# wq's load cut into 16 and 112 partitions in a one-token decode kernel

## The chip, the cores and the metric

The kernel runs on one core of a Trainium2 chip. Five engines of the core take part: TensorE (PE), VectorE (DVE), ScalarE (ACT), GpSimd (POOL) and SyncE (SP). Sixteen DMA engines move data between the device memory and the core's memory of 128 partitions (SBUF). The metric is the device time of one execution in microseconds, the median of the runs; a profiled execution gives the trace.

## What is computed

Two sequences, one new token each (B = 2, Sq = 1, D = 512). A grouped attention over a cached context of 32,768 positions, and a small MLP whose result gates it:

```python
xn = layernorm(x)
q  = (xn @ wq)                  # 32 heads of 128, 8 of them in keys and values: 4 heads share one
p  = softmax(q . k_cache * 128**-0.5)
s  = (p . v_cache) @ wo
h  = mlp_in_and_shift(layernorm(xn), w1) @ w2    # the shifts leave only zeros where S = 1
x1 = xn + h
g  = silu(x1 + gelu(layernorm(x1) @ w3) @ w4)
out = x + s * g
```

All inputs are bf16. With one token, each shifted group of the MLP's first part is padded with zeros alone, so that w1 and w2 do not reach the result and the kernel does not load them. What has to be moved is the cache, 2 x 8 pairs of K and V of 8 MiB each (268 MB), and the weights: wq 4 MiB, w3 and w4 1.75 MiB each, wo 4 MiB.

## The kernel before

Two large buffers hold what is loaded. `kbuf` has three places of 32 KB a partition (`CW` elements each), `vbuf` two. A K tile takes two of kbuf's three places, and the tiles of even and odd units overlap in the middle one. At the start kbuf's third place holds wq and vbuf's first 28 KB hold w3; both are used up before K of unit 1 and the first half of V of unit 0 arrive in their place.

There are 16 units n (sequence n % 2, key head n // 2). For each, `scores` lets DVE transpose K in eight pieces (L488), and PE multiplies each by the unit's q (L500); `softmax` follows on DVE, PE and ACT (L513 to L530); `values` multiplies the probabilities by V on PE (L541), and `unit_sum` and `unit_out` collect the result. At the end come the gelu, w4, wo and the gate.

Ahead of the units, `q_job` makes q for all heads: PE multiplies xrep (the normalised x, spread over the array) by wq in 32 matmuls (L448), ACT copies the eight results out (L458), DVE transposes them (L463) and packs them into qp (L465), and POOL places a unit's part into qz (L474). `mlp_in` (L572) follows on PE and reads w3. xrep comes from x through the two layernorms, a pair of small loads (z4) and a transpose (L426, L429).

All instructions are recorded in one list an engine by the class `Plan`, which works out the waits: each operation names the regions that it reads and writes, and where two overlap, the later one waits for the semaphore of the earlier. A load adds 16 to its semaphore when it has landed. SP issues all the large loads in program order on one queue: wq, w3, the two halves of K of unit 0, the second half of V of unit 0 (L326 for each, which is the helper's line), then the first half of V after `mlp_in` has read w3, and from there K and V of the next unit as soon as their places have been read. ACT issues the four small loads of x and z4 on a queue of its own.

The first loads are written so:

```python
wq_v = A_wq.rearrange("(p k) f -> p k f", k=DK)
wq_s = kbuf[:, 2 * CW:3 * CW].rearrange("p (k f) -> p k f", k=DK)
load("wq", wq_s, wq_v, [kreg(2 * CW, CW)])
load("w3", w3_s, w3_v, [("vbuf", 0, W3)])
load_k(0)
load_v0_half(1)
```

Each partition's part of wq is 32 KB in one piece, on both sides.

Of the kernel before, what the change touches and what calls it, by code (L numbers as in the profile page):

```python
# [195 lines left out]
def kernel(  # L196
# [37 lines left out]
    CW = UT * Dh  # L234
# [4 lines left out]
    wq_v = A_wq.rearrange("(p k) f -> p k f", k=DK)  # L239
# [6 lines left out]
    def sb(name, shape, dt, align=32):  # L246
        return nc.alloc_sbuf_tensor(name, shape, dt, align_bytes=align).ap()
# [12 lines left out]
    xrep = sb("xrep", [128, DK, 4, 32], BF16)  # L260
# [52 lines left out]
    def al(name, lo=0, hi=1 << 30):  # L313
        return (name, lo, hi)

    def on(eng):
        def record(fn, rd=(), wr=(), label=None, times=None):
            P.op(eng, fn, [al(r) if isinstance(r, str) else r for r in rd],
                 [al(w) if isinstance(w, str) else w for w in wr], label=label, times=times)
        return record  # L320

    dve, act, pool, pe = on("DVE"), on("ACT"), on("POOL"), on("PE")

    def load(sem, out_ap, in_ap, wr, rd=(), eng="SP"):
        e = {"SP": nc.sync, "ACT": nc.scalar}[eng]
        P.op(eng, lambda: e.dma_start(out=out_ap, in_=in_ap), [al(r) if isinstance(r, str) else r for r in rd],  # L326
             [al(w) if isinstance(w, str) else w for w in wr], dma=sem)
# [10 lines left out]
    def kreg(lo, w):  # L338
        return ("kbuf", lo, lo + w)
# [18 lines left out]
    wq_s = kbuf[:, 2 * CW:3 * CW].rearrange("p (k f) -> p k f", k=DK)  # L358
    w3_s = vbuf[:, 0:W3].rearrange("p (k f) -> p k f", k=DK)
    w4_s = kbuf[:, 0:FK * D].rearrange("p (f d) -> p f d", f=FK)  # L360

    load("wq", wq_s, wq_v, [kreg(2 * CW, CW)])
    load("w3", w3_s, w3_v, [("vbuf", 0, W3)])
    load_k(0)

# [67 lines left out]
    def q_job():  # L433
        kb = kbuf[:, :]

        q_row, q_turn = (vbuf[:, W3 + HD * i:W3 + HD * (i + 1)] for i in range(2))

        def vreg(i, lo, w):
            return ("vbuf", W3 + HD * i + lo, W3 + HD * i + lo + w)

        spots = [("sc", 0, 512), ("sc", 512, 1024), "acc", "mA", "hP", "mD", "wP", "s_ps"]

        def fn(done):

            pes = [mybir.EngineType.PE]
            with nc.Fori(0, 2, 1, engines=pes) as e, nc.Fori(0, 4, 1, engines=pes) as h:
                for k in range(DK):
                    r = T.matmul(  # L448
                        banks[:, bass.ds(e * 2048 + h * 512, 512)],
                        lhsT=xrep[:, k, :, :].rearrange("p i w -> p (i w)"),  # L450
                        rhs=kb[:, bass.ds(h * 1024 + (e + (2 * CW + k * HD)), 1023)][:, 0:1023:2],
                        start=(k == 0), stop=(k == DK - 1))
                done(r)

        for c, spot in enumerate(spots):
            pe(None if c else fn, [kreg(2 * CW, CW), "xrep"], [spot], times=None if c else 8)
        for c, spot in enumerate(spots):
            act(lambda c=c: A.copy(  # L458
                out=q_row.rearrange("p (h x two w) -> p h two x w", h=4, two=2, w=32)[:, c % 4, c // 4, :, :],
                in_=banks[:, 512 * c:512 * (c + 1)].rearrange("p (x w) -> p x w", w=32)),  # L460
                [spot], [vreg(0, 1024 * (c % 4) + 512 * (c // 4), 512)])
        for c in range(0, 4096, 1024):
            dve(lambda c=c: V.transpose(out=q_turn[:, c:c + 1024], in_=q_row[:, c:c + 1024]),  # L463
                [vreg(0, c, 1024)], [vreg(1, c, 1024)])
        dve(lambda: V.tensor_copy(  # L465
            out=qp[:, :, :, :, :].rearrange("p k b g h -> p k b (g h)"),
            in_=q_turn.rearrange("p (h k b c) -> p k b h c", k=4, b=B, c=16)[:, :, :, :, 0]), [vreg(1, 0, HD)], ["qp"])

        for t, name in ((acc, "acc"), (mD, "mD"), (wP, "wP")):
            dve(lambda t=t: V.memset(t, 0.0), [], [name])  # L470
# [109 lines left out]
    def gelu():  # L580
# [9 lines left out]
        dve(lambda: V.transpose(out=h_bf[:, :], in_=h_row[:, :]), ["h_row"], ["h_bf"])  # L590

    q_job()
    place_q(0)
    mlp_in()
# [138 lines left out]
```

## Time and profile before

| | |
|---|---|
| median of 3 runs | 657.31 us (656.68 to 657.52) |
| profiled execution | 656.69 us, of which the span of the instructions 654.9 us |
| PE, DVE, ACT busy | 61%, 59%, 5% of the span |
| DMA | 280.55 MB, mean 428 GB/s over the span |
| mean granted clock of TensorE | 0.834 |

The profile is one execution, taken by the hardware profiler. Its page gives the busy time of each engine, the span in 40 slices, the DMA queues (q1 is SP's, q10 ACT's), the chain of work that ended last, the costliest groups of instructions by line, and the DMA issues with the time from issue to landing. The timeline lists instructions in order: start, duration, engine (SPq is SP's queue, where a duration is that of the issue), line, what is written and read, and in brackets how long the engine stood idle before and what ended that. Busy time by stretch gives for each stretch its length, the busy time and count of each engine, the granted clock, the share of the 16 DMA engines and their rate in GB/s.

### The profile page before, as it was taken

The page shows a single profiled execution, that of the slowest core. Times are in us where ns is not written, and L with a number is a line of the kernel's source. Part 1 is how long each engine was busy: PE and PEld are TensorE (multiplying, and loading weights), DVE is VectorE, ACT ScalarE, POOL GpSimd, SP SyncE. Part 2 cuts the span into 40 slices and gives each one's busy share as a digit, 9 for nine tenths or more (in the row PEclk, how much of TensorE's full clock was granted, in tenths as well). Part 3 has the DMA queues.
Part 4 walks back from the last instruction along what each step waited for, and adds up shares of the span by engine and source line. Part 5 has one row for each costly group of instructions (what it writes and reads, how often), then busy time and mean ns, then how long its engine had stood idle before and what let it go on. Part 6 is the DMA issues. An engine that isn't in the chain of part 4 may idle for free.

```text
span 654.9 us, 5862 instructions
## 1 busy us (share of the span) xinstructions
PE 397.9 (61%) x2297; PEld 152.0 (23%) x2297; DVE 384.6 (59%) x302; ACT 33.5 (5%) x67; POOL 7.6 (1%) x28
## 2 busy tenths in 40 slices
PE   0876183665648466573855658486464847646855
PEld 0222031221213222121321213122121312212322
DVE  4592381945739185572928548293763819367862
ACT  1201000000000000000000000000000000000011
POOL 1000000000000000000000000000000000000000
PEclk9997598886979878697887869787797977779988
DMA  8999999999999999999999999999999999999996
GB/s 360 448 424 466 400 448 444 448 416 420 448 444 436 404 444 444 448 416 420 448 444 444 396 445 444 448 424 412 448 444 444 404 436 444 448 428 406 450 411 278
DMA packets 6383, 280.55 MB, mean 428 GB/s; under 512 B 738, under 2 KB 748, under 8 KB 1260
## 3 DMA queue, kind: packets, MB, share of 16 engines
q1 hardware_dynamic: 6348, 280.50, 99.1%
q8 instruction: 2, 0.03, 0.0%
q10 hardware_dynamic: 32, 0.01, 0.0%
q14 instruction: 1, 0.01, 0.0%
HBM read 280.50 MB, written 0.00 MB: 428 GB/s over the span
## 4 chain that ended last, share of the span: by engine, by line
DMA 73%; DVE 14%; PE 7%; issue 5%; SPq 0%; DVEq 0%
DMA kbuf<-in_A_k_cache_dram 69%; DVE ktb L488 13%; PE banks L500 7%; DMA kbuf<-in_A_wo_dram 5%; DVE acs L551 1%; SPq L326 0%; DVE acr L555 0%; DVEq L90 0%; PE banks L654 0%; DVE sg L688 0%; DVE out_bf L689 0%; SPq L728 0%; SPq L693 0%
## 5 line engine op out<-in xcount | busy, mean ns | idle before, releaser
L488 DVE STREAM_TRANSPOSE ktb<-kbuf 128x2048 uint32<-128x2048 uint32 x128 | 286.8, 2286 | 172.9 <-DMA kbuf<-in_A_k_cache_dram 170.7
L500 PE MATMUL banks<-ktb,qz 128*128 128x512 bf16 x1024 | 268.2, 410 | 164.8 <-DVE ktb L488 164.1
L500 PEld LDWEIGHTS banks<-ktb,qz 128*128 128x128 bf16 x1024 | 95.6, 102 | 338.6 <-issue 189.6
L541 PE MATMUL banks<-vbuf,pT 128*16 128x512 bf16 x1024 | 90.6, 532 | 15.9 <-DVE rS L530 13.1
L541 PEld LDWEIGHTS banks<-vbuf,pT 128*16 128x16 bf16 x1024 | 31.8, 117 | 68.0 <-issue 56.8
L513 DVE TENSOR_REDUCE m<-banks 128x1 f32<-128x1024 f32 x16 | 19.6, 1225 | 32.0 <-PE banks L500 32.0
L529 DVE STREAM_TRANSPOSE pT<-pr 128x1024 bf16<-128x1024 bf16 x16 | 19.9, 1245 | 20.4 <-ACT pr L523 20.4
L565 ACT CAST oQ<-banks 128x4 bf16<-128x4 f32 x16 | 2.6, 162 | 519.8 <-PE banks L562 519.8
L526 PE MATMUL banks<-S,headf 128*128 128x1 f32 x32 | 7.8, 314 | 23.8 <-ACT pr L523 23.8
L448 PE MATMUL banks<-kbuf,xrep 128*128 x32 | 10.4, 480 | 16.8 <-DVE xrep L429 16.3
L523 ACT ACTIVATE pr<-banks,nb 128x1024 bf16<-128x1024 f32 x16 | 17.8, 1114 | 39.0 <-DVE nb L522 39.0
L555 DVE TENSOR_REDUCE acr<-acs 128x128 f32<-128x512 f32 x17 | 17.6, 1036 | 0.6
L514 PE MATMUL banks<-identf,m 128*1 128x128 f32 x16 | 4.3, 270 | 19.2 <-DVE m L513 19.2
L551 DVE SCALAR_TENSOR_TENSOR acs<-banks,rS,mask 128x512 f32<-128x512 f32 x17 | 12.1, 711 | 5.3 <-PE banks L541 5.3
L519 PE MATMUL banks<-ones_f,gx 1*128 1x1 f32 x32 | 6.4, 266 | 9.9 <-DVE gx L517 9.9
L526 PEld LDWEIGHTS banks<-S,headf 128*128 128x128 f32 x32 | 6.5, 252 | 25.2 <-ACT pr L523 25.2
L474 POOL TENSOR_TENSOR qz<-qp,qm 128x64 bf16<-128x64 bf16 x17 | 5.0, 293 | 621.3 <-PE banks L500 595.3
L463 DVE STREAM_TRANSPOSE vbuf<-vbuf 128x1024 bf16<-128x1024 bf16 x4 | 4.9, 1234 | 8.6 <-ACT vbuf L458 8.5
L448 PEld LDWEIGHTS banks<-kbuf,xrep 128*128 128x128 bf16 x32 | 3.6, 113 | 23.1 <-issue 21.4
L519 PEld LDWEIGHTS banks<-ones_f,gx 1*128 1x128 f32 x32 | 5.0, 196 | 13.0 <-DVE gx L517 13.0
L515 DVE TENSOR_REDUCE gm<-banks 1x4 f32<-1x128 f32 x16 | 4.5, 278 | 5.8 <-PE banks L514 5.8
L522 DVE TENSOR_SCALAR nb<-banks 128x1 f32<-128x1 f32 x16 | 2.5, 158 | 7.8 <-PE banks L519 7.8
(74 smaller groups left out, 61.0 us busy)
## 6 DMA issues: line engine op xcount, KB each, us to landing
kbuf<-in_A_k_cache_dram SPq DMA_DIRECT2D x4, 4096.0 KB, 27.0
vbuf<-in_A_v_cache_dram SPq DMA_DIRECT2D x2, 4096.0 KB, 35.6
kbuf<-in_A_wq_dram SPq DMA_DIRECT2D x1, 4096.0 KB, 13.4
kbuf<-in_A_wo_dram SPq DMA_DIRECT2D x1, 2048.0 KB, 33.6
vbuf<-in_B_w_dram SPq DMA_DIRECT2D x1, 1792.0 KB, 17.2
kbuf<-in_B_w_dram SPq DMA_DIRECT2D x1, 1792.0 KB, 29.9
kbuf<-in_A_wo_dram SPq DMA_DIRECT2D x1, 1024.0 KB, 32.1
kbuf<-in_A_wo_dram SPq DMA_DIRECT2D x4, 256.0 KB, 30.9
```

The source lines that it names most:

```text
L448: r = T.matmul(banks[:, bass.ds(e * 2048 + h * 512, 512)], lhsT=xrep[:, k, :, :].rearrange("p i w -> p (i w)"), rhs=kb[:, bass.ds(h * 1024 ...
L474: pool(lambda: G.tensor_tensor(out=qz[:, :, 32 - rep:].rearrange("p k (i w) -> p k i w", w=32)[:, :, :, 0:rep], in0=qp[:, :, b, g, :].unsq ...
L488: dve(lambda i=i, c0=c0: V.transpose(out=ktb[i][:, :], in_=kbuf[:, c0:c0 + KG * GT * Dh].bitcast(U32)), [kreg(c0, KG * GT * Dh)], [f"ktb{i ...
L500: r = T.matmul(sc[:, bass.ds(half, HW)].rearrange("p (t k) -> p t k", k=32), lhsT=qz[:, k, off:off + 128], rhs=kv[:, k // 2, k % 2, :, :], ...
L513: dve(lambda: V.tensor_reduce(out=m1[:, :], in_=sc[:, :], axis=AX.X, op=ALU.max), ["sc"], ["m1"], "max")
L519: pe(lambda: T.matmul(bc, lhsT=gx[:, :, :].rearrange("o x h -> o (x h)"), rhs=ones_f[0:1, 0:1], start=True, stop=True), ["gx", "ones_f"], ...
L523: act(lambda: A.activation(out=pr[:, :], in_=sc[:, :], func=ACT.Exp, bias=nb[:, 0:1], scale=inv_sqrt_dh, accum_out=S1[:, :]), ["sc", "nb"] ...
L526: pe(lambda: T.matmul(sS, lhsT=headf[:, :, :].rearrange("p x h -> p (x h)"), rhs=S1[:, :], start=True, stop=True), ["headf", "S1"], [rO], "S")
L529: dve(lambda: V.transpose(out=pT[:, :, :].rearrange("p t r -> p (t r)"), in_=pr[:, :]), ["pr"], ["pT"], "pT")
L541: r = T.matmul(acc[32 * j:32 * j + 16, :].rearrange("p (i d) -> p i d", d=Dh), lhsT=pT[:, half * GT + u, r0:r0 + 16], rhs=vv[:, x, u, :, : ...
L551: dve(lambda: V.scalar_tensor_tensor(out=acs[:, :, :], in0=acc[:, :].rearrange("p (i d) -> p i d", d=Dh), scalar=rS[:, 0:1], in1=mask[:, : ...
L555: dve(lambda: V.tensor_reduce(out=acr[:, :], in_=acs[:, :, :].rearrange("p i d -> p d i"), axis=AX.X, op=ALU.add), ["acs"], ["acr"], "acr")
```

## The change

The one load of wq becomes two on the same semaphore: the first 16 partitions, then the other 112. The first writes the region of kbuf as before; the second is recorded as writing a name of its own, "wq_rest", so that it does not wait for the first. The q matmuls name both, and so wait until the semaphore stands at 32 where it was 16. SP issues one instruction more; the lists of the other engines have the same instructions as before, and what SP issues after it keeps its order.

```diff
-    load("wq", wq_s, wq_v, [kreg(2 * CW, CW)])
+
+    for p0, p1, spot in ((0, 16, kreg(2 * CW, CW)), (16, 128, "wq_rest")):
+        load("wq", wq_s[p0:p1], wq_v[p0:p1], [spot])
     load("w3", w3_s, w3_v, [("vbuf", 0, W3)])
     load_k(0)
...
         for c, spot in enumerate(spots):
-            pe(None if c else fn, [kreg(2 * CW, CW), "xrep"], [spot], times=None if c else 8)
+            pe(None if c else fn, [kreg(2 * CW, CW), "wq_rest", "xrep"], [spot], times=None if c else 8)
```

## The prediction

> **What bounds the kernel now.** I read the page first (span, the DMA strip, the chain that ended last), then the chain in order of time, then busy time by stretch, and last the timeline of the first 45 us.
>
> ```profile
> span 654.9 us, 5862 instructions
> DMA  8999999999999999999999999999999999999996
> DMA packets 6383, 280.55 MB, mean 428 GB/s; under 512 B 738, under 2 KB 748, under 8 KB 1260
> q1 hardware_dynamic: 6348, 280.50, 99.1%
> DMA 73%; DVE 14%; PE 7%; issue 5%; SPq 0%; DVEq 0%
> ```
>
> The 16 DMA engines are busy in every slice but the first and the last, nearly all of it with the one queue of SP (q1), and the chain is 73% transfers. The rest of the chain, the DVE and PE pieces, could still be time in which the DMA engines stand still. The next view says that it is not.
>
> ```profile
> core 0: us, PE busy (x) PEld busy (x) DVE busy (x) ACT busy (x) POOL busy (x), PEclk, DMA share, GB/s
> 1.75:2.75 1.00, 0.00 (x0) 0.00 (x0) 0.20 (x1) 0.20 (x1) 1.00 (x5) 1.00 1.96 526
> 2.75:3.75 1.00, 0.00 (x0) 0.00 (x0) 1.00 (x1) 1.00 (x1) 0.82 (x1) 1.00 0.00 0
> 3.75:4.75 1.00, 0.00 (x0) 0.00 (x0) 0.93 (x3) 0.09 (x1) 0.00 (x0) 1.00 1.22 524
> 12.00:40.00 28.00, 18.07 (x67) 5.62 (x68) 16.67 (x17) 4.69 (x8) 0.30 (x1) 1.00 1.01 436
> 100.00:600.00 500.00, 310.05 (x1751) 119.22 (x1752) 294.30 (x207) 17.62 (x38) 3.52 (x12) 0.82 1.00 433
> ```
>
> The last column is the rate of the transfers. From 12 us on it is 436, and over the 500 us of the middle 433 GB/s: one rate, without pauses. 280.5 MB at 433 GB/s take 648 us of the 654.9; the other 7 us are the start and the end. So the transfers' stream bounds the kernel, and a microsecond lost or won in it is lost or won in the span, if the stream has always work in its queue. It has:
>
> ```profile
> 2.37 35.56 DMA kbuf<-in_A_k_cache_dram
> 41.69 34.90 DMA kbuf<-in_A_k_cache_dram
> 512.87 27.37 DMA kbuf<-in_A_k_cache_dram
> 619.89 31.13 DMA kbuf<-in_A_wo_dram
> 651.07 0.32 PE banks L654 x8
> ```
>
> A K load has 8.39 MB, 19.4 us at 433 GB/s. The one issued at 512.87 lands 27.37 us later, so 8.0 us of other work stood ahead of it; at 41.69 it was 34.90 - 19.4 = 15.5 us. The chain names the DVE between two K loads because DVE's reads release the next issue, but each issue comes 8 us or more before the engines need it. At the end PE needs 0.3 us after the last part of wo has landed: nothing there gives time back.
>
> **The change, part by part.** It cuts the first transfer of the program (wq, 128 partitions of 32 KB each) in two: partitions 0 to 15, then 16 to 127. Bytes, later loads and the instructions of the compute engines stay. One issue is added on SP, and the wait of PE ahead of the q matmuls counts both loads.
>
> ```profile
> 0.96 0.39 SPq L326 DMA_DIRECT2D kbuf<-in_A_wq_dram  x1
> 1.42 0.41 SPq L326 DMA_DIRECT2D vbuf<-in_B_w_dram  x1
> 2.90 28.17 SPq L326 DMA_DIRECT2D vbuf<-in_A_v_cache_dram  x2
> 14.35 0.38 DVE L425 CAST zb<-z 128x256 bf16<-128x256 f32 x1 [4.64 <-DMA z<-ktb]
> 15.25 0.29 DVE L429 COPY xrep<-zT 128x512 bf16<-128x512 bf16 x1
> 16.26 8.22 PE L448 MATMUL banks<-kbuf,xrep 128*128 x24 [16.26 <-DVE xrep L429]
> 31.06 4.47 DVE L488 STREAM_TRANSPOSE ktb<-kbuf 128x2048 uint32<-128x2048 uint32 x2
> 41.69 0.33 SPq L326 DMA_DIRECT2D kbuf<-in_A_k_cache_dram  x1
> kbuf<-in_A_wq_dram SPq DMA_DIRECT2D x1, 4096.0 KB, 13.4
> ```
>
> *One more issue on SP.* Two issues stand 1.42 - 0.96 = 0.46 us apart. The rest of wq, w3, both halves of K and the first half of V are issued 0.46 us later. The cover is the first row of each engine: 524 KB, 16 rows of 32 KB, at 433 GB/s are 1.21 us a row, and the first rows took about 2 (begun from 1.75 on, the second ones from 3.75 on, in the rows above). 0.46 is less than either, so I cost it at 0; without the cover it would be +0.46. The ACT queue's loads (x, x4, z4) are not behind it.
>
> *The start.* By quarters of a microsecond the first rows begin so:
>
> ```profile
> 1.75:2.00 0.25, 0.00 (x0) 0.00 (x0) 0.00 (x0) 0.00 (x0) 0.25 (x2) 1.00 1.08 270
> 2.00:2.25 0.25, 0.00 (x0) 0.00 (x0) 0.00 (x0) 0.00 (x0) 0.25 (x3) 1.00 5.02 1311
> 2.25:2.50 0.25, 0.00 (x0) 0.00 (x0) 0.00 (x0) 0.00 (x0) 0.25 (x1) 1.00 0.95 262
> 2.50:2.75 0.25, 0.00 (x0) 0.00 (x0) 0.20 (x1) 0.20 (x1) 0.25 (x2) 1.00 0.78 262
> ```
>
> A quarter at 262 GB/s is 65.5 KB, two rows; so 2, 10, 2 and 2 engines begin in the four quarters (the strip puts a packet's bytes where it begins). The four late ones are up to 0.75 us behind the first. A first load with one row for each engine may let them all begin together. That is worth 0 to 0.75 us, and only if a late one is also the one that ends last; I take -0.3.
>
> *The first 16 rows.* No row of this trace shows sixteen engines writing into sixteen neighbouring partitions, so I bound it. A single row is no limit: an engine puts 32 KB into one partition in 1.21 us. The 16 engines together write no faster than 16 rows in 1.21 us, and whether neighbours share a way into the memory can't be seen, since each load spreads over all 128 partitions. If no neighbours share, the 16 rows cost 1.21 us as now: +0. If the eight partitions that fall to an engine now (128 / 16) were neighbours with one way for all, 16 neighbours would have two ways and the rows would queue eight deep: 8 x 1.21 - 1.21 = +8.5 us for every engine. Between the ends lie two to a way (+1.2) and four to a way (4 x 1.21 - 1.21 = +3.6). The rows don't single one out, and the middle of the two ends, 4.2, is nearest to four to a way: I take +3.6 and keep both ends.
>
> [...]
>
> *The other 112 rows.* Seven rows for each engine, 7 x 1.21 = 8.5 us, as the last seven of eight now: +0 at best. At worst, in runs of seven, every row meets another engine's row on one way: 7 x 1.21 = +8.5. In the present load nobody waits (1.21 us a row, in the rate of 433 GB/s). Seven is no multiple of two, four or eight, so runs of seven would not line up with ways of that many neighbours, and some rows meet; the slowest engine counts, since a load has landed when its last engine is done. Nearest to the known end of no meeting I take one and a half rows, +1.8.
>
> *Does the lost time come back?* The sum so far makes the last engine 5.1 us late at the end of wq, and the rates above show no spare speed to catch up with. What waits for wq is PE at L448. wq lands at 0.96 + 13.4 = 14.4 and PE starts at 16.26, released by xrep (15.25 + 0.29); so 1.9 us are hidden, and with wq 5.1 us later PE starts about 3.2 us later. Behind it on PE wait the w3 matmuls, after them SP's issue of V's second half (the 28.17 us at 2.90 end at 31.07), and through q the transposes at 31.06 and the K issue at 41.69. All shift by some 3 us against 15.5 us of queued transfers: hidden. If that cover were gone, 3.2 us would be added instead of hidden. The z4 load, which lands at 14.35, has its rows among wq's and may be some late too; it shares the same cover.
>
> *Sum:* 0 - 0.3 + 3.6 + 1.8 = +5.1 us. The profiled execution took 656.69 us beside its span of 654.9; 656.69 + 5.1 = 661.8. It lies 0.6 under the median of the runs, 657.31, so the runs should give about 657.31 + 5.1 = 662.4 us, 0.8% slower. What a measurement of this kernel can tell from no change is about 0.2%, 1.3 us.
>
> **The rivals.**
>
> *The rows do not hinder each other and only the start counts.* Then 656.6 to 657.3 us: the -0.3 taken, at most -0.75. It decides when neighbours have ways of their own. For it: one row at a time runs at full rate into one partition. Against it: nothing in this trace, where no load is so narrow. Within 0.2%. To be faster by over 0.2% also the slow first rows have to shrink: 2.0 - 1.21 = 0.8 and the 0.75 of the spread, together -1.5 us, 655.8. The 2 us are the same for early and late engines, which speaks for a latency that a smaller load pays as well.
>
> *The small load isn't one row for each engine.* If an engine is tied to its partitions, 16 neighbours fall to few of the engines, and the others begin at once with the rest; each engine has its eight rows in all, as before, and the time is 657.3. For it: now every engine gets eight rows and none waits. [...]
>
> *The rest is dealt in turn, row by row.* Then each of its seven steps again puts 16 neighbours side by side, and each costs what the first 16 rows cost: 8 x 3.6 = +29 us, 686. Nothing in the trace shows how rows are dealt. With eight to a way in the first load alone, +8.5 + 1.8 - 0.3, it would be 667.3.
>
> **How the numbers follow.** Slower by 2 to 9 us through the narrow load: 0.57, its own range 659.5 to 666.5 (first load at two to eight rows deep, the rest at 0 to three rows). Much slower (rest in turn, or eight to a way): 0.09. No hindrance: 0.19 within 0.2% and 0.05 faster. Few engines: 0.10, same. That is faster 0.05, same 0.29, slower 0.66. The likeliest gives 662.4. With signs on both sides, a range for 8 in 10 must reach from the unhindered cases, 656.6, over the likeliest one's upper end to 667.0; outside are the 0.09, the 0.05 and a few hundredths of the edges.
>
> **What would show it.** Right: between about 2 and 7 us the rate falls to 100 to 200 GB/s, where it is now 526, 0 and 524 in single microseconds; wq lands near 19 us (its last part 18 after its issue); L448 starts near 19.5 released by the wq load and not by xrep; the middle stays at 433 GB/s; each K landing, and the last of wo, about 5 us later. Wrong: second rows starting from 3.75 to 4.75 as now. If the first rows show 5 us and wq lands 4 late but the span grows less, the stream had slack that I did not see; if it grows by far more than wq is late, some engines ran dry, or the wait at L448 reached the K issue.

## The result and the profile after

The changed kernel took 665.39 us, the median of 4 runs (664.53 to 665.86), against 657.37 for the kernel before in the same sitting: 8.0 us more, a ratio of 1.0126 with a 95% interval of 1.0114 to 1.0138. The forecast was 662.4 with a range of 656.6 to 667.0. Two of the four runs of `probe_far`, below, took 736.6 us at a lower granted clock (0.79 to 0.80, where its other two had 0.82); they are left out and not explained.

The profiled execution took 665.81 us, its span is 664.0. The page of the changed kernel: span, DMA strip, rates in 40 slices (GB/s), and the chain by engine and by line.

```profile
span 664.0 us, 5863 instructions
DMA  9999999999999999999999999999999999999996
GB/s 209 350 436 444 442 438 442 430 442 403 434 442 442 438 442 430 442 403 434 442 438 442 442 427 442 407 434 442 438 442 442 426 442 407 434 442 430 450 399 285
DMA 70%; DVE 14%; PE 10%; issue 5%; SPq 0%; DVEq 0%; ACT 0%
```

The second row says "busy" from the first slice to the last, and the third says that in the first slice and a half the busy engines moved less than they do later (the first two slices had 360 and 448 GB/s in the kernel before). The share counts the engines as busy whether they move much or little (1.07 at 172 GB/s and 1.01 at 254 in the rows of the changed kernel below), so the strip of shares hides the loss and the rate shows it.

Busy time by stretch, of the kernel before:

```profile
2.00:8.00 6.00, 0.00 (x0) 0.00 (x0) 4.67 (x13) 2.31 (x4) 1.57 (x4) 1.00 1.07 413
8.00:22.00 14.00, 5.74 (x15) 2.09 (x16) 2.69 (x13) 1.58 (x3) 0.00 (x0) 1.00 1.00 429
22.00:24.00 2.00, 1.98 (x10) 0.72 (x8) 0.00 (x0) 1.34 (x3) 0.00 (x0) 1.00 0.83 360
24.00:100.00 76.00, 45.76 (x229) 16.41 (x227) 50.18 (x36) 4.58 (x9) 0.88 (x3) 0.84 1.02 440
```

and of the changed kernel:

```profile
1.75:2.00 0.25, 0.00 (x0) 0.00 (x0) 0.00 (x0) 0.00 (x0) 0.25 (x2) 1.00 0.71 135
2.00:2.25 0.25, 0.00 (x0) 0.00 (x0) 0.00 (x0) 0.00 (x0) 0.25 (x3) 1.00 9.44 1311
2.25:2.50 0.25, 0.00 (x0) 0.00 (x0) 0.00 (x0) 0.00 (x0) 0.25 (x1) 1.00 4.46 659
2.50:2.75 0.25, 0.00 (x0) 0.00 (x0) 0.12 (x1) 0.20 (x1) 0.25 (x2) 1.00 0.00 0
2.75:4.75 2.00, 0.00 (x0) 0.00 (x0) 1.93 (x3) 1.09 (x1) 0.81 (x1) 1.00 0.00 0
2.00:8.00 6.00, 0.00 (x0) 0.00 (x0) 4.59 (x13) 2.31 (x4) 1.56 (x4) 1.00 1.07 172
8.00:22.00 14.00, 0.00 (x0) 0.00 (x0) 1.57 (x10) 0.00 (x0) 0.00 (x0) 1.00 1.01 254
22.00:24.00 2.00, 0.00 (x0) 0.00 (x0) 1.12 (x3) 0.00 (x0) 0.00 (x0) 1.00 0.84 330
24.00:100.00 76.00, 48.91 (x220) 17.40 (x221) 43.42 (x32) 7.33 (x12) 0.59 (x2) 0.80 1.01 438
100.00:600.00 500.00, 310.76 (x1750) 119.07 (x1748) 293.78 (x208) 17.77 (x39) 3.80 (x13) 0.82 1.00 434
```

From 24 us on the two kernels move data equally fast (440 and 438 GB/s up to 100 us). Before that, the changed one lacks (413 - 172) x 6 = 1,446 KB between 2 and 8 us, (429 - 254) x 14 = 2,450 KB between 8 and 22, and 60 KB after. At 433 GB/s these are 3.3 + 5.7 + 0.1 = 9.1 us, and the two spans are 664.0 - 654.9 = 9.1 us apart. (The two profiled executions lie at the outer ends of their runs; the medians are 8.0 apart.) So all the time went into the 22 us in which wq is loaded, and none came back. The first rows do begin more evenly: none after 2.50 us, where before two began after 2.50. But then no second row begins until after 4.75 us.

Share and rate together give the mean time of a row of 32 KB on an engine. Between 8 and 22 us it is 1.01 x 16 x 32.8 KB / 254 GB/s = 2.1 us in the changed kernel, and 1.00 x 16 x 32.8 KB / 429 GB/s = 1.2 us in the kernel before. The trace also has each packet's own time: of the 95 rows of 32 KB that begin between 8 and 20 us in the changed kernel, the quickest took 1.64 us and the slowest 2.40; the 98 of the kernel before took 1.21 each. So it is not that some of the rows were held up; every one of these was.

The changed kernel's timeline and chain around q, and the last transfer:

```profile
0.95 0.86 SPq L326 DMA_DIRECT2D kbuf<-in_A_wq_dram  x2
22.16 0.39 DVE L427 CAST zb<-z 128x256 bf16<-128x256 f32 x1 [12.45 <-DMA z<-ktb]
24.63 9.53 PE L450 MATMUL banks<-kbuf,xrep 128*128 x28 [24.63 <-DMA kbuf<-in_A_wq_dram]
1.42 22.39 DMA kbuf<-in_A_wq_dram
50.77 34.98 DMA kbuf<-in_A_k_cache_dram
629.04 31.11 DMA kbuf<-in_A_wo_dram
```

wq is in at 1.42 + 22.39 = 23.81, where it was 14.4. The q matmuls start at 24.63 in place of 16.26, now released by wq. The small z4 load lands 7.8 us later too. The K issue at 41.69 has moved to 50.77; its load takes 34.98 us to land, as before (34.90), so as much work was queued ahead of it. wo's last part lands at 660.15 in place of 651.02.

### The profile page after: what moved, and what is told of

Read it like the earlier page. It is cut to its first block, busy times and chain, and to the rows that moved or that the text cites. A ratio compares the mean times of both kernels' runs of the same rounds, so it can differ in the third digit from the quotient of the medians.

```text
span 664.0 us, 5863 instructions
## 1 busy us (share of the span) xinstructions
PE 401.8 (61%) x2297; PEld 152.9 (23%) x2297; DVE 384.8 (58%) x302; ACT 33.5 (5%) x67; POOL 7.6 (1%) x28
## 4 chain that ended last, share of the span: by engine, by line
DMA 70%; DVE 14%; PE 10%; issue 5%; SPq 0%; DVEq 0%; ACT 0%
DMA kbuf<-in_A_k_cache_dram 62%; DVE ktb L490 13%; PE banks L502 8%; DMA kbuf<-in_A_wo_dram 5%; DMA kbuf<-in_A_wq_dram 3%; PE banks L450 1%; DVE vbuf L465 1%; DVE acs L553 0%; DVE acr L557 0%; SPq L326 0%; DVE banks L472 0%; DVEq L90 0%; ACT vbuf L460 0%; PE banks L656 0%; DVE sg L690 0%
## 5 line engine op out<-in xcount | busy, mean ns | idle before, releaser
L502 PE MATMUL banks<-ktb,qz 128*128 128x512 bf16 x1024 | 271.6, 414 | 161.7 <-DVE ktb L490 161.0
L543 PE MATMUL banks<-vbuf,pT 128*16 128x512 bf16 x1024 | 91.1, 534 | 15.9 <-DVE rS L532 13.1
L450 PE MATMUL banks<-kbuf,xrep 128*128 x32 | 10.5, 490 | 25.0 <-DMA kbuf<-in_A_wq_dram 24.6
L450 PEld LDWEIGHTS banks<-kbuf,xrep 128*128 128x128 bf16 x32 | 3.7, 115 | 31.4 <-issue 29.8
```

What stands on the lines that cost most here:

```text
L450: r = T.matmul(banks[:, bass.ds(e * 2048 + h * 512, 512)], lhsT=xrep[:, k, :, :].rearrange("p i w -> p (i w)"), rhs=kb[:, bass.ds(h * 1024 ...
L502: r = T.matmul(sc[:, bass.ds(half, HW)].rearrange("p (t k) -> p t k", k=32), lhsT=qz[:, k, off:off + 128], rhs=kv[:, k // 2, k % 2, :, :], ...
L543: r = T.matmul(acc[32 * j:32 * j + 16, :].rearrange("p (i d) -> p i d", d=Dh), lhsT=pT[:, half * GT + u, r0:r0 + 16], rhs=vv[:, x, u, :, : ...
```

## The experiments

Each kernel was timed beside the kernel before on the same chip. "Over before" is the difference of the two medians.

| kernel | median, us | over before |
|---|---|---|
| the change: 16 + 112 partitions | 665.39 | +8.0 |
| cols: 128 partitions twice, cut along the row | 656.98 | -0.1 |
| late_q: q held back, no transfer changed | 660.27 | +3.2 |
| probe_near: 16 rows more, partitions 0 to 15, ahead of wq | 660.73 | +3.6 |
| probe_far: the same, partitions 0, 8, ..., 120 | 658.8, 659.0 | +1.8 |
| probe_near_src: as probe_near, rows read from apart | 660.83 | +3.7 |
| probe_112: 112 rows more, partitions 16 to 127 | 673.05 | +15.9 |
| halves: wq as 0 to 63, 64 to 127 | 666.72 | +9.6 |
| oddeven: wq as even, odd partitions | 656.86 | -0.3 |
| mid_step1: 16 rows more behind wq, partitions 0 to 15 | 662.91 | +6.0 |
| mid_step2, mid_step4, mid_step8: the same, 2, 4, 8 apart | 660.76, 660.67, 661.10 | +3.8, +3.7, +4.1 |

**Two loads, or narrow loads?** `cols` keeps two loads on one semaphore, and the q matmuls that wait for both, but leaves both loads as wide as the array.

```diff
-    load("wq", wq_s, wq_v, [kreg(2 * CW, CW)])
+    for k0, k1, spot in ((0, 1, kreg(2 * CW, CW)), (1, DK, "wq_rest")):
+        load("wq", wq_s[:, k0:k1], wq_v[:, k0:k1], [spot])
```

> wq in two loads, but cut along the row: both write all 128 partitions, first 8 KB of each partition's 32 KB, then the other 24 KB. If the narrowness of the two loads costs the 8 us (theory: neighbouring partitions share a way into the memory), this costs nothing: 656.5 to 658, xrep ready and PE at the q matmuls near 16.3 us. If two loads in place of one cost it (the added issue, the dealing of the rows to the engines), it is as slow as the changed kernel, 664 to 666.

656.98 against 657.10 us, ratio 0.9998 (0.9989 to 1.0007): the first figure. `cols`, by stretch:

```profile
2.00:8.00 6.00, 0.00 (x0) 0.00 (x0) 4.96 (x13) 2.30 (x4) 1.57 (x4) 1.00 1.04 407
8.00:22.00 14.00, 5.26 (x17) 1.90 (x17) 2.70 (x13) 2.34 (x4) 0.00 (x0) 1.00 1.03 441
```

The rates are near those of the kernel before (413 and 429). The second issue and the second load cost nothing that can be measured, so the 8 us hang on the partitions that each load covers.

**Is it the late q?** PE's and DVE's pieces around q had entered the chain, so a delay of the computation had to be told from a delay of the transfers. `late_q` leaves every load as it was and holds the q matmuls back until half of K is there.

```diff
-            pe(None if c else fn, [kreg(2 * CW, CW), "xrep"], [spot], times=None if c else 8)
+            pe(None if c else fn, [kreg(2 * CW, CW), kreg(CW, CW), "xrep"], [spot], times=None if c else 8)
```

> The kernel before, with the q matmuls also waiting for the first half of K to land (about 28 us), so they start some 12 us later than now and 3.5 us later than in the changed kernel; no transfer changes. If the span follows the stream of transfers alone, this is hidden by the 15.5 us of queued work: 656.7 to 658. If the late start of q is what costs in the changed kernel, it costs here more than there: 666 to 670.

660.27 us against 657.10, ratio 1.0047 (1.0031 to 1.0062): neither figure. The trace of `late_q` (chain, SP's queue, stretches):

```profile
55.29 21.74 DMA kbuf<-in_A_k_cache_dram
77.44 0.33 SPq L326 DMA_DIRECT2D vbuf<-in_A_v_cache_dram  x1
60.00:74.00 14.00, 9.14 (x55) 4.01 (x57) 7.39 (x8) 2.65 (x4) 0.29 (x1) 0.83 0.94 407
74.00:80.00 6.00, 3.73 (x46) 1.35 (x39) 2.95 (x2) 0.00 (x0) 0.00 (x0) 0.84 0.74 273
```

With everything behind q 13.6 us later (the K issue at 55.29, before 41.69), the K load lands at 77.03 and the next V load is issued only at 77.44: for a moment the queue of transfers is empty, and the rate falls to 273 GB/s. Against 433 the two stretches lack 14 x 26 + 6 x 160 = 1,324 KB, 3.1 us, which is the 3.2 that it costs. So the cover is smaller than the 15.5 us that I read from the K load; the V issue of unit 1 is the tight one. The changed kernel issues that V load at

```profile
72.94 0.33 SPq L326 DMA_DIRECT2D vbuf<-in_A_v_cache_dram  x1
```

12.8 us ahead of the landing of its K load (50.77 + 34.98 = 85.75), because its transfers are late as well. There is no such hole in it (438 GB/s from 24 to 100 us), and the late q is not what costs there.

**The first 16 rows alone.** The next kernels keep wq's load whole and add one of 16 rows of 32 KB, on a semaphore of its own, whose destination V overwrites later. The bytes, 524 KB at 433 GB/s, cost 1.2 us; the rest is the price of the form. `probe_near` and `probe_far` differ in the destination only, `probe_near_src` in the source only.

```diff
+    load("pb", vbuf[0:16, CW:2 * CW].rearrange("p (k f) -> p k f", k=DK), wq_v[0:16], [("vbuf", CW, 2 * CW)])
     load("wq", wq_s, wq_v, [kreg(2 * CW, CW)])
# probe_far:       vbuf[0:128:8, ...], wq_v[0:16]
# probe_near_src:  vbuf[0:16, ...],    wq_v[0:128:8]
```

> The kernel before with one load more ahead of wq: 16 rows of 32 KB (a copy of wq's first 16) into 16 neighbouring partitions of a place that V overwrites later. Its bytes alone cost 1.2 us. Theory (neighbours share ways): the rows take about 4 us as in the changed kernel, so 1.2 + 1.8 to 3.6, 660.4 to 662.2. If a narrow load by itself costs nothing and only the 112-row load does: 658.6.

> The same added load of the same 16 rows, now into every eighth partition (0, 8, ..., 120). Theory: neighbours no longer share a way, or at most two rows do, so 1.2 to 2.4 us over before, 658.6 to 659.8, and clearly less than with neighbouring partitions. If it is the reading of one 512 KB piece, or the small load itself, that is slow, as with neighbouring partitions: 660.4 to 662.2.

> The added load into 16 neighbouring partitions once more, but its 16 rows read from every eighth row of wq instead of from one 512 KB piece. If the writing side is what is slow: as the added load into neighbours, 660.2 to 661.3. If the reading of neighbouring rows is: 658.3 to 659.3.

`probe_near` 660.73 us (ratio 1.0056, 1.0040 to 1.0071): 2.4 us beyond its bytes. `probe_far` 658.8 and 659.0, two runs and so without an interval: 0.6 beyond its bytes, and below the lowest run of `probe_near`, 660.4. `probe_near_src` 660.83 (1.0054, 1.0037 to 1.0071): as `probe_near`. First `probe_near`, then `probe_far`:

```profile
2.00:8.00 6.00, 0.00 (x0) 0.00 (x0) 4.29 (x13) 2.30 (x4) 1.57 (x4) 1.00 1.10 243
8.00:22.00 14.00, 2.86 (x7) 1.04 (x8) 2.69 (x13) 0.58 (x1) 0.00 (x0) 1.00 0.99 424
```

```profile
2.00:8.00 6.00, 0.00 (x0) 0.00 (x0) 4.95 (x13) 2.31 (x4) 1.57 (x4) 1.00 1.05 342
8.00:22.00 14.00, 4.45 (x11) 1.62 (x12) 2.69 (x13) 1.17 (x2) 0.00 (x0) 1.00 1.00 431
```

Only the stretch with the small load is slow, 243 GB/s for neighbours and 342 for partitions eight apart. It is the writing side, and the distance of the partitions counts. From where the rows are read does not count in the time (660.83 against 660.73 us).

**The 112 rows alone.** The same place, partitions and rows 16 to 127.

> The kernel before with a load of 112 rows of 32 KB into partitions 16 to 127 of that same place, ahead of wq's whole load. Its bytes alone cost 3.67 MB / 433 GB/s = 8.5 us: 665.6 if 112 rows are as fast as 128. The added load into 16 neighbours cost 3.6 us with its bytes, 2.4 without; the changed kernel lost 8.0, so 5.6 are left for the 112 rows. If they are slow by themselves: 657.1 + 8.5 + 4.5 to 6.5, 670 to 672.

673.05 us, 1.0238 (1.0221 to 1.0255): 15.9 over before, 7.4 us beyond the 8.5 for the bytes, and 1 us above the forecast of a load that is slow by itself. `probe_112`:

```profile
2.00:8.00 6.00, 0.00 (x0) 0.00 (x0) 4.96 (x13) 2.30 (x4) 1.56 (x4) 1.00 1.17 320
8.00:22.00 14.00, 0.00 (x0) 0.00 (x0) 2.69 (x13) 0.00 (x0) 0.00 (x0) 1.00 0.94 265
```

265 GB/s from 8 to 22 us, much as in the changed kernel (254). A load of 112 partitions is slow by itself, with nothing narrow ahead of it, and it is the larger part of the loss. It cost more than the 5.6 that the difference between the changed kernel and `probe_near` had left for it.

**Which 64 partitions.** wq once more in two loads, both of 64 partitions, one kernel for each of the two added lines; the q matmuls wait for both loads.

```diff
-    load("wq", wq_s, wq_v, [kreg(2 * CW, CW)])
+    for p0, p1, step, spot in ((0, 64, 1, kreg(2 * CW, CW)), (64, 128, 1, "wq_rest")):      # halves
+    for p0, p1, step, spot in ((0, 128, 2, kreg(2 * CW, CW)), (1, 128, 2, "wq_rest")):      # oddeven
+        load("wq", wq_s[p0:p1:step], wq_v[p0:p1:step], [spot])
```

> wq in two loads of 64 partitions, 0 to 63 and 64 to 127. If each engine takes a run of neighbouring rows (four here) and the ways are used in between by all, each load leaves half of the ways unused, two engines meet on each way in use, and each of the eight rows takes up to twice 1.21 us: up to +9.7, 662 to 667. If rows are dealt to the engines in turn, 16 neighbours are written at a time as in the first 16 rows, now in all eight steps: 676 to 687. If loads of this width are free: 657.

> wq in two loads of 64 partitions, the even ones, then the odd ones. Over a whole load all the ways are used evenly. If it counts that a load as a whole reaches all the ways, this costs little, 657 to 659; if it counts which rows are under way at the same moment, engines still meet (even partitions in runs of four rows to an engine span eight partitions, and every second group of neighbours is idle at a time): 660 to 667, like the halves.

`halves` 666.72 us (1.0143, 1.0126 to 1.0160), `oddeven` 656.86 (0.9996, 0.9986 to 1.0006). First `halves`, then `oddeven`:

```profile
2.00:8.00 6.00, 0.00 (x0) 0.00 (x0) 4.89 (x13) 2.31 (x4) 1.56 (x4) 1.00 1.20 259
8.00:22.00 14.00, 0.00 (x0) 0.00 (x0) 1.56 (x10) 0.00 (x0) 0.00 (x0) 1.00 0.92 190
```

```profile
2.00:8.00 6.00, 0.00 (x0) 0.00 (x0) 4.74 (x13) 2.30 (x4) 1.56 (x4) 1.00 1.00 380
8.00:22.00 14.00, 5.65 (x14) 2.03 (x15) 2.69 (x13) 1.48 (x3) 0.00 (x0) 1.00 1.01 434
```

Over 2 to 22 us `halves` moves (259 x 6 + 190 x 14) / 20 = 211 GB/s, half of 433, and pays the 9.7 us that halving the rate for the 9.7 us of wq must cost (+9.6). `oddeven`, with loads of the same width, pays nothing. So the 64 partitions are not slow for being fewer than 128 (434 GB/s from 8 to 22 us in `oddeven`); they are slow when they lie together (190 in `halves`).

**How far apart.** The added load of 16 rows once more, now behind wq, in the running stream. In the changed kernel the load of 16 rows began them all by 2.50 us and ended with sixteen packets of four bytes, which speaks for one row to each engine; if that holds here, the price tells how many rows share a way.

> The added load of 16 rows of 32 KB, now behind wq, in the running stream, into partitions 0 to 15. One row goes to each engine, so the time of the rows shows how many engines share a way. Ways of four neighbours: 1.2 for the bytes + 3.6, 661.9. Ways of eight neighbours: 1.2 + 8.5, 666.8. As at the start of the program (2.4 without the bytes): 660.7.

> The same into every second partition, 0 to 30. Ways of four neighbours: two to a way, 1.2 + 1.2, 659.5. Ways of eight neighbours: four to a way, 1.2 + 3.6, 661.9.

> The same into every fourth partition, 0 to 60. Ways of four neighbours, all separate: 1.2, 658.3; if partitions 32 apart share a way as well, two to a way, 659.5, as with every second partition. Ways of eight neighbours: two to a way, 659.5.

> The same into every eighth partition, 0 to 120. Ways of eight neighbours or of four: all separate, 658.3. If partitions 32 apart share a way: two to a way, 659.5.

The medians over before are 6.0, 3.8, 3.7 and 4.1 us (ratios 1.0092, 1.0060, 1.0059 and 1.0065, each within 0.0018): 4.8 beyond the bytes for neighbours, 2.5 to 2.9 for the others. The stretch from 10 to 24 us, in `mid_step1`, `mid_step8` and the kernel before:

```profile
10.00:24.00 14.00, 3.85 (x10) 1.36 (x11) 1.12 (x3) 0.81 (x2) 0.00 (x0) 1.00 1.01 312
```

```profile
10.00:24.00 14.00, 5.42 (x18) 1.99 (x18) 1.12 (x3) 2.34 (x4) 0.00 (x0) 1.00 1.01 387
```

```profile
10.00:24.00 14.00, 7.72 (x23) 2.81 (x24) 1.12 (x3) 2.92 (x5) 0.00 (x0) 1.00 0.99 427
```

The rates lack (427 - 312) x 14 = 1,610 KB, 3.7 us at 433 GB/s, and (427 - 387) x 14 = 560 KB, 1.3 us. Steps 2 and 4 show 387 too. Those are the prices that the forecast worked out for four rows to a way (3.6) and two to a way (1.2). The medians lie 1.1 to 1.6 us above. The rate is a mean over the engines, and the end waits for the last of them. The trace's packets show the difference: each large load ends with sixteen packets of four bytes (704 for the 44 of the kernel before), as many as there are engines. For the first half of K of unit 0 they begin between 26.28 and 27.88 us in the kernel before, between 31.18 and 34.04 in `mid_step1` and between 28.96 and 31.90 in `mid_step8`. In the mean that is 5.1 and 2.9 us later, near the bytes and the missing rate (1.2 + 3.7 and 1.2 + 1.3); for the last packet it is 6.2 and 4.0, as the medians (6.0 and 4.1). So the added load left the engines further apart, and the span follows the last one.

That four and eight apart are no better than two apart (387 GB/s in all three) speaks against ways of plain neighbours alone: with ways of four, every fourth partition would have been free, 658.3 us by the forecast, and `mid_step4` took 660.67. What is left of the forecasts is a sharing that also puts two rows to a way at four and at eight apart (659.5). The rates fit it; no run shows it by itself.

One thing is not shown: the equal price of the three spread sets would also come out if any load of 16 rows in the running stream cost 1.3 us, or if its rows met rows of the loads before and behind it. A load of 16 rows in the same place, into partitions that share no way, would tell; which partitions those are, no run shows, and that kernel was not run.

## Why the prediction was right, and where not

The direction, the range and the cause hold: the span follows the stream of transfers, the narrow loads make it slower on the writing side, and what is lost is not regained. 662.4 was 3.0 us short, 5.1 for 8.0. It would have been further off if the errors of the two main terms had not partly cancelled: the first load cost 1.2 us less than its term and the rest 3.8 more. That part is luck. By its steps:

- *What bounds the kernel.* Right: the missing bytes between 2 and 24 us, divided by 433 GB/s, are the difference of the spans.
- *One more issue on SP, 0.* Right (`cols`, -0.1, by its interval between -0.7 and +0.5).
- *The start, -0.3.* The first rows began more evenly, as supposed. That it is worth anything is not shown: `cols`, which also begins with a small load, is no faster. Nor are the 2 us of the first rows the same for early and late ones: in the kernel before they took 1.34 to 2.40, and the last to begin took the 1.34.
- *The first 16 rows, +3.6.* The size fits: in the running stream the rate lacks 3.7 us (`mid_step1`). That four rows share a way is my reading of it; in the changed kernel the first 16 rows took 2.78 to 4.18 us each, and four times 1.21 is 4.84. And the term was the case nearest to the middle of two bounds and came from no row, so that it met the 3.7 is in part luck. At the start of the program, as here, they cost less, 2.4 (`probe_near`); the added load behind wq cost 4.8. Why the place counts is not shown.
- *The other 112 rows, +1.8.* This is the step that was mis-sized: 8.0 - 2.4 = 5.6 us in the changed kernel, if the prices of the two loads add, and 7.4 alone (`probe_112`). I let some rows meet and took one and a half rows' time; 5.6 are 4.6 rows' time, within the end of +8.5. All the rows were slowed, to about 2.1 us from 1.21, and seven (112 / 16) times 0.8 to 0.9 us is 5.6 to 6.3. Why they were is not shown. My guess is that it hangs on which rows stand side by side at one moment, and so on how the 112 rows are dealt to the engines: the trace doesn't give the partition of a row, and the cause of this size stays open. Dealing in turn, which would have cost 29 us, is excluded as it stood.
- *The cover of the late q.* Hidden in the changed kernel, as forecast, but the cover was misread. PE started 8.4 us later, not 3.2, since wq and z4 were later, and `late_q` shows that 13.6 us of delay cost 3.2. I took the cover from the K load; the V issue is nearer the edge.
- *The likeliest case's own range.* 659.5 to 666.5 doesn't follow from what stands beside it: two rows deep and no meeting is -0.3 + 1.2 = +0.9 us, 658.2, and eight deep with three rows -0.3 + 8.5 + 3.6 = +11.8, 669.1. The 4.6 rows of the second load lie outside its zero to three; the total is inside because the first load was cheaper.
- *The signs.* The rate between 2 and 8 us was 172 GB/s, in the 100 to 200 given, the middle kept its rate, and L448 (L450 in the changed kernel) was released by the wq load. But wq landed at 23.81 and not near 19, and wo's last part 9.1 us later and not 5. The lateness of wq carried over whole: wq landed 9.4 us later, the profiled span grew by 9.1.
- *The rivals.* "No hindrance" fell with `probe_near` against `probe_far`. "Few engines" fell as well: 16 rows began between 1.75 and 2.50 us, and no second one until after 4.75, and the load ended with sixteen packets of four bytes (4.77 to 6.35 us), so none of the engines had the rest to go on with.

## What to carry to other kernels

Where the transfers bound a kernel, as here, the partitions that a load covers are part of its price: 64 partitions side by side ran at half the rate (211 GB/s against 433), 64 every second one at the full rate (434), and 112 of 128 were slower than all 128 (254 to 265 against 429). If a load is to be cut so that something small comes first, cut it along the row and keep all the partitions in each piece (`cols`: 656.98 against 657.10 us). Look for such a loss in the rate, not in the share: the engines counted as busy (1.01) at 254 GB/s as at 429 (1.00).

## What was not expected

112 partitions, all but 16, ran at 254 to 265 GB/s in the stretch from 8 to 22 us, against 429 for 128; by the count of partitions alone it would be an estimated 375 (429 x 112 / 128). And 64 partitions two apart lost nothing (-0.3 us), though 16 rows put two apart into the running stream cost 2.6 us beyond their bytes. The two loads differ in the number of rows, in their place in the stream and in the partitions they span (0 to 126 and 0 to 30); which of these makes the difference, no run shows. How the rows of a load are dealt to the engines was not seen here, and for the 112 it is the open question.
